# Spreading a first mixture's eighths over an attention loop, and preparing the second mixture as soon as its expert order is known

## Chip, cores and metric

One Trainium2 chip, one of its cores. The metric is the device time of one execution in microseconds; the time before is the median of three runs.

## What is computed

Attention over 4 batches of 8 heads (576 positions, 64 wide) in which each query keeps its 32 largest scores, then a gated feed-forward layer ("the first mixture" below, 512 to 2048 to 512), then a layer of 8 experts ("the second mixture", 512 to 1024 to 512) in which each of the 2304 tokens goes through the one expert that a router picks for it.

```python
scores = scale * np.matmul(q, k.transpose(0, 1, 3, 2))
kth = np.partition(scores, -top_k, axis=-1)[..., -top_k:-top_k + 1]
scores = np.where(scores >= kth, scores, -1000000000.0)
attn = softmax(scores); x = attn @ v                      # -> 2304 x 512
h = x @ w_in; g = h * np.clip(h + 3.0, 0.0, 6.0) / 6.0    # first mixture
x = g @ w_out
expert_idx = np.argmax(xn @ en.T / tau, axis=1)           # router
h = np.maximum(x[mask] @ w1[e], 0.0)                      # second mixture, per expert
out[mask] = gate_w[mask, None] * (h @ w2[e])
```

## The kernel before

Attention runs in 72 units of 128 query rows of two heads (or of left-over rows of four heads: units 8, 13, 26, 31, 44, 49, 62, 63). A software pipeline written by hand takes one **step** (`step`, L751) per unit, 76 in all. In step i, TensorE makes the scores of unit i, VectorE picks the 32 largest of unit i-1 (`select`, the many MAX8 and MATCH_REPLACE8), ScalarE and GpSimd mask and exponentiate units i-2 and i-3, and TensorE transposes unit i-4 and multiplies it with its values (`turned`, `values`). Inside the loop the order of instructions on each engine is the order of the calls in `step`; each engine takes its own in order, and so does the queue of DMA issues on SyncE (the SP queue). The last operation on VectorE that belongs to the scores of a unit is L360, one per step; below, "step s" in a trace is the stretch from the L360 of step s to that of step s+1.

The first mixture is done in groups of one or two 128-token tiles as soon as their attention is finished (`push_group`). The first two groups have one tile, the other eight have two. A group is cut into eight **eighths** of the hidden width, queued in `moe`. An eighth is a first product (L508, 24 matmuls), gate (ScalarE), swish (VectorE, L518), `large` and `small` (a value split in a high and a low part, ScalarE and GpSimd), and a second product (L541, 6 matmuls a tile). Groups become ready in steps 7, 11, 21, 29, 39, 47, 57, 65, 75, and a last group, the left-over rows, after the loop. `step` takes eighths from `moe`: one a step, but two (`a` and `b`) in one step as long as they are of one-tile groups. So before, the one-tile groups run in steps 8 to 15, steps 16 to 21 have no eighth, the two-tile groups run in steps 22-37, 40-55 and 58-73, and steps 38, 39, 56, 57, 74, 75 have none. The last two groups run after the loop.

Weights of the first mixture arrive as 64-bit numbers and are put together from two 32-bit words in 32 conversions (`convert_w`, called by `words` up to four times a step). Each result is split into a high part that stays in SBUF and a low part that is written to DRAM (L218, `lo_dram`) and fetched again for every eighth (`fetch`, L227: 512 KB for each product). A conversion fetches its next raw pieces (L181). Before, steps 0-3 make two conversions each, 4-7 three, 8-10 four.

After a group's second product the tile's rows go to DRAM (`y_dram`, L552) and four small pieces of routing work are queued in `side` (`route`: r1, r2, r4, r5). When 16 of the 18 tiles are routed, `order` (L644 on) ranks the experts by their token counts. `ahead` then prepares the first expert of the second mixture: it loads that expert's token list (`idt`, L692) and weights (L697, L706), gathers its first 256 tokens from `y_dram` (L726, `tokens`), transposes them (L730) and splits the weights (L710, L711). The second mixture follows, with its first product in L901. After the loop the order of instructions is a scheduler's, by simulated times and priorities.

```python
        while moe or last or side:
            if not moe and not rest and "order" in late and "w1" not in late:
                at.close()
                ahead()
            if side:
                with tc.high_priority(offset=SIDE):
                    side.popleft()()
            last = whole(moe.popleft() if moe else None, last)
```

So before, `ahead` is called when the last group's eighths have all been taken, and its gather reads `y_dram` after the last group's rows have been written there.

Of the kernel before, what the change touches and what calls it, by code (L numbers as in the profile page):

```python
# [35 lines left out]
NUNIT = 72  # L36
NS = 4
EARLY = 9
HS = S // 2
QS = S // 4  # L40
SCALE = 1.0 / 8.0
# [2 lines left out]
SIDE = 100  # L44
# [22 lines left out]
def layers(ctx: ExitStack, tc: tile.TileContext, qt, kt, v, w_in, w_out, embt, tau, w1, w2, out, y_dram, g_dram, x_dram, tbl, lo_dram, flag):  # L67
# [71 lines left out]
    def setup():  # L139
        nc.vector.memset(ones, 1.0)  # L140
        nc.vector.memset(acc, 0.0)
        nc.gpsimd.iota(iota8, pattern=[[1, 8]], base=0, channel_multiplier=0, allow_small_or_imprecise_dtypes=True)
        nc.gpsimd.iota(ebase, pattern=[[STRIDE, 8]], base=0, channel_multiplier=0, allow_small_or_imprecise_dtypes=True)
        nc.gpsimd.affine_select(tri, ones, pattern=[[1, 128]], compare_op=ALU.is_gt, fill=0.0, base=0, channel_multiplier=-1)
        nc.gpsimd.iota(ids[:, :, 0], pattern=[[128, NG]], base=0, channel_multiplier=1)
        nc.gpsimd.iota(ids[:, 0:16, 1].rearrange("p (b t) -> p b t", b=4), pattern=[[S, 4], [128, 4]], base=0, channel_multiplier=1)
        for hf in range(2):
            nc.gpsimd.iota(ids[64 * hf:64 * hf + 64, 16:18, 1], pattern=[[2 * S, 2]], base=hf * S + 512, channel_multiplier=1)
        padt = mp.tile([128, E * STRIDE * 2 // 128], I32, tag="ug", name="padt", bufs=4)
        nc.gpsimd.memset(padt, PAD)  # L150
        nc.sync.dma_start(out=tbl.rearrange("(p a) b -> p (a b)", p=128), in_=padt)
        zr = mp.tile([128, DM], F32, tag="ug", name="zr", bufs=4)
        nc.vector.memset(zr, 0.0)
        nc.sync.dma_start(out=y_dram[NT:NT + 1, :], in_=zr[0:1, :])
        for g in (14, 15):
            nc.sync.dma_start(out=y_dram[128 * g:128 * g + 128, :], in_=zr)
        nc.sync.dma_start(out=g_dram[NT:NT + 128, :].rearrange("p o -> o p"), in_=zr[0:1, 0:128])

# [64 lines left out]
    def fetch(n, m):  # L223

        if m < total and m not in lows_[n]:
            lows_[n][m] = t = lop.tile([128, 1024], F32R, tag=f"l{n}", name=f"lo{n}")
            nc.sync.dma_start(out=t.bitcast(F32), in_=lo_dram[n][m % 8])  # L227
# [257 lines left out]
    moe = deque()  # L485
    side = deque()
# [146 lines left out]
    late = {}  # L633
# [118 lines left out]
    def step(i, last):  # L752
# [1 line left out]
            if 0 <= i - j < NU:  # L754
                f(i - j, *a)

        more = iter(range(2 if i < 4 else 3 if i < 8 else 4))

        def words():
            if next(more, None) is not None:  # L760
                convert_w()


        a = moe.popleft() if moe else None
        b = moe.popleft() if moe and a[7] == moe[0][7] == 1 else None
        if last and not last[2]:
            part(last[0], 4)
            part(last[0], 5)
# [30 lines left out]
        at_(3, inverse)  # L799
        if i - 3 >= EARLY:  # L800
            at_(3, scale)
# [27 lines left out]
            setup()  # L829
        if i == 5:  # L830
            embed()
        words()
        return (b, None, False) if b else (a, None, True) if a else None

    if True:
# [18 lines left out]
        last = last[0] if last else None  # L854
        rest = True
        while moe or last or side:
            if not moe and not rest and "order" in late and "w1" not in late:
                at.close()
                ahead()
            if side:  # L860
                with tc.high_priority(offset=SIDE):
                    side.popleft()()
            last = whole(moe.popleft() if moe else None, last)
            if rest and len(moe) <= 1:
                rest = False
                finish_rest()
# [108 lines left out]
        more = nc.values_load(ordi[0:1, 2 * E + 1:2 * E + 2], min_val=0, max_val=NT)  # L975
# [96 lines left out]
```

## Time and profile before

| | |
|---|---|
| median of 3 runs | 1235.53 us (1234.05 to 1240.3) |
| profiled execution | 1232.73 us, span 1230.9 us |
| PE / VectorE / ScalarE / GpSimd busy | 1042.4 / 841.9 / 727.6 / 658.5 us |
| steps 0 to 21 end (L360 of step 22) | 319.7 us |
| L360 of step 71, the last | 789.9 us |
| last matmul of the first mixture issued | 917.29 us |

Times in the trace are microseconds from the span's start. PE is TensorE, DVE VectorE, ACT ScalarE, POOL GpSimd, SPq the DMA queue of SyncE. In a timeline row the bracket tells how long the engine stood idle before the instruction and what ended that; a busy PE is pipelined and its ends are modelled, so it need not be at its peak.

### The profile page before, as it was taken

The numbers are of one execution on the slowest core, as the hardware profiler recorded it, in microseconds if no ns is written. First come the engines' busy times: TensorE is split into PE (matmuls) and PEld (weight loads), VectorE is DVE, ScalarE is ACT, GpSimd is POOL, SyncE is SP. The second block draws the span as 40 slices with busy tenths as digits, with TensorE's granted clock in tenths as the row PEclk, the third lists the DMA queues.
The fourth block names the chain that finished last, engine by engine and source line by source line (L and its number), as shares of the span: only waits on it lengthen the run. The fifth ranks groups of instructions, "written<-read, shape, count | busy, mean of one in ns | idle before, by whom it ended". The sixth has DMA issues, their size and how long they took to land. (4 is left out here: it accounts for less than half of the span.)

```text
span 1230.9 us, 22028 instructions
## 1 busy us (share of the span) xinstructions
PE 1042.4 (85%) x7416; PEld 909.0 (74%) x7416; DVE 841.9 (68%) x2720; ACT 727.6 (59%) x1520; POOL 658.5 (53%) x868
## 2 busy tenths in 40 slices
PE   2333588986999998999998999999976888999993
PEld 1233577974888886888877888879866777888882
DVE  6978576689988999998999898821234343444440
ACT  5656466677777787777887777652333343344540
POOL 6867465577766687766887666642211243122200
PEclk9999878987999998999999999999997999999997
DMA  7645565742433555344454245336670563244530
GB/s 241 200 134 174 195 226 168 230 137 83 145 117 102 170 152 170 83 153 153 119 179 140 86 129 173 112 112 202 190 240 19 170 209 120 85 179 166 184 145 21
DMA packets 99427, 184.98 MB, mean 150 GB/s; under 512 B 21391, under 2 KB 47138, under 8 KB 99295
## 3 DMA queue, kind: packets, MB, share of 16 engines
q1 hardware_dynamic: 94655, 173.29, 43.8%
q0 software_dynamic: 4640, 10.10, 2.5%
q8 instruction: 63, 1.03, 0.4%
q14 instruction: 69, 0.57, 0.2%
HBM read 164.26 MB, written 19.71 MB: 149 GB/s over the span
## 5 line engine op out<-in xcount | busy, mean ns | idle before, releaser
L508 PE MATMUL bank_h<-xh,lo 128*128 128x256 f32 (+1 forms) x640 | 184.7, 289 | 20.7 <-DMA lo<-lo_dram 20.7
L396 POOL TENSOR_TENSOR s<-s,z 128x576 f32<-128x576 f32 x144 | 185.9, 1291 | 11.6 <-ACT z L392 10.0
L508 PE MATMUL bank_h<-xh,vh 128*128 128x256 f32 (+1 forms) x640 | 189.2, 296 | 3.2 <-DVE u L518 3.2
L508 PE MATMUL bank_h<-xl,vh 128*128 128x256 f32 (+1 forms) x640 | 184.4, 288 | 1.1 <-DVE xl L465 1.1
L375 DVE MAX8 A<-left 128x8 f32<-128x288 f32 (+1 forms) x288 | 160.2, 598 | 0.0
L508 PEld LDWEIGHTS bank_h<-xh,lo 128*128 128x128 f32 x640 | 126.8, 198 | 21.4 <-DMA lo<-lo_dram 21.4
L514 ACT ACTIVATE u<-bank_h,half 128x512 f32<-128x512 f32 (+1 forms) x80 | 51.6, 645 | 149.1 <-PE bank_h L508 140.8
L429 PE MATMUL bank_t<-ident,s 128*128 128x128 f32 x648 | 109.2, 298 | 35.6 <-ACT pt L434 12.3
L525 POOL TENSOR_TENSOR gl<-u,gh 128x512 fp32r<-128x512 f32 (+1 forms) x80 | 95.1, 1189 | 80.6 <-ACT gh L522 79.7
L508 PEld LDWEIGHTS bank_h<-xh,vh 128*128 128x128 f32 x640 | 126.6, 198 | 9.0 <-DVE u L518 4.5
L344 PE MATMUL ps_sc<-kst,qh 128*128 128x288 f32 x256 | 88.8, 359 | 51.3 <-ACT s L347 23.2
L508 PEld LDWEIGHTS bank_h<-xl,vh 128*128 128x128 f32 x640 | 126.8, 198 | 1.9 <-DVE xl L465 1.3
L518 DVE SCALAR_TENSOR_TENSOR u<-u,bank_h 128x512 f32<-128x512 f32 (+1 forms) x80 | 50.5, 632 | 110.3 <-ACT u L514 91.1
L541 PE MATMUL y<-lo,gh 128*128 128x512 f32 x288 | 115.4, 401 | 12.4 <-DMA lo<-lo_dram 12.4
L541 PE MATMUL y<-wh,gh 128*128 128x512 f32 x288 | 119.8, 416 | 0.0
L429 PEld LDWEIGHTS bank_t<-ident,s 128*128 128x128 f32 x648 | 78.1, 150 | 52.3 <-ACT pt L434 23.3
L434 ACT COPY pt<-bank_t 128x384 f32<-128x384 f32 x216 | 96.1, 480 | 31.7 <-PE bank_t L429 30.4
L392 ACT ACTIVATE z<-s,zb 128x576 bf16<-128x576 f32 x144 | 112.9, 784 | 1.9 <-DVE zb L381 1.9
L541 PE MATMUL y<-wh,gl 128*128 128x512 f32 x288 | 113.5, 400 | 0.2 <-POOL gl L525 0.2
L402 ACT ACTIVATE s<-s,nb 128x576 f32<-128x576 f32 x144 | 111.9, 777 | 0.0
L711 DVE TENSOR_TENSOR l<-a,h 128x1024 fp32r<-128x1024 f32 x64 | 76.5, 1222 | 50.9 <-ACT h L710 44.3
L447 PE MATMUL bank_a<-pt,vt 128*64 128x128 f32 (+1 forms) x1600 | 104.6, 284 | 0.6 <-ACT pt L434 0.6
(228 smaller groups left out, 2830.0 us busy)
## 6 DMA issues: line engine op xcount, KB each, us to landing
lo<-lo_dram SPq DMA_DIRECT2D x160, 512.0 KB, 4.2
a<-in_moe_w_dram SPq DMA_DIRECT2D x64, 512.0 KB, 7.4
kraw<-in_k_dram SPq DMA_DIRECT2D x64, 144.0 KB, 2.5
qraw<-in_q_dram SPq DMA_DIRECT2D x64, 128.0 KB, 3.2
w<-in_moe_w_in_dram SPq DMA_DIRECT2D x32, 256.0 KB, 3.3
w<-in_moe_w_out_dram SPq DMA_DIRECT2D x32, 256.0 KB, 3.1
lo_dram<-wf SPq DMA_DIRECT2D x32, 256.0 KB, 2.0
vt<-in_v_dram SPq DMA_DIRECT2D x16, 320.0 KB, 3.5
```

The costliest lines, as they stand in the source:

```text
L344: nc.tensor.matmul(ps[:, n, :HS], t, kk[:, HS * g:HS * g + HS], start=(o == 0), stop=(o == len(parts) - 1))
L375: nc.vector.max(A[:, n, 8 * r:8 * r + 8], src[:, n, :w])
L392: nc.scalar.activation(zb_[n], tile_of(i, n), AF.Relu, bias=sel[i][2][:, n:n + 1], scale=-BIG)
L396: nc.gpsimd.tensor_tensor(s, s, zb_[n], op=ALU.subtract)
L402: nc.scalar.activation(s, s, AF.Exp, bias=sel[i][1][:, n:n + 1], scale=SCALE, accum_out=sums[i][:, n:n + 1])
L429: nc.tensor.transpose(pp[:, 128 * k:128 * k + 128], e[:, 128 * (3 * c + k):128 * (3 * c + k) + 128], ident)
L434: nc.scalar.copy(pts[i][:, 3 * c:3 * c + 3, :].rearrange("p k n -> p (k n)"), tb_.pop((i, c))[:, :384])
L447: nc.tensor.matmul(av[64 * n:64 * n + 64, c0:c1], vt[:, k, 64 * n:64 * n + 64], pt[:, k + 5 * n if k < 4 else 4, c0:c1], start=(o == 0), s ...
L508: nc.tensor.matmul(ph[:, a, :], w, x[:, k, :], start=(k == 0 and n == 0), stop=(k == 3 and n == 2))
L525: nc.gpsimd.tensor_tensor(state[q][1], state.pop((q, "u")).rearrange("p (a n) -> p a n", a=2), state[q][0].bitcast(F32), op=ALU.subtract)
L541: nc.tensor.matmul(state["y"][o], x[:, a, c], w, start=(f == 0 and n == 0), stop=(f == 15 and n == 2))
L711: nc.vector.tensor_tensor(lo, x, hi.bitcast(F32), op=ALU.subtract)
```

## The change

A table of steps replaces the rule by group size: one eighth a step, two in steps 18 and 20, none in steps 26, 35, 44, 53, 62, 71. The one-tile groups then run in steps 8 to 21, and the others in steps 22-30 (less 26), 31-39 (less 35), and so on to 75. Conversions go at 2, 2, 3 in turn, and end in step 13. The first two fetches are made in step 6. After the loop two pieces of routing are taken per turn in place of one, and `ahead` is called as soon as the order is known, while eighths are still queued; the zeros that `y_dram` is given at the start are now in tiles 16 and 17, the last group's.

```diff
+PAUSE = tuple(range(26, 72, 9))
+TWO = (18, 20)
...
-        for g in (14, 15):
+        for g in (16, 17):
             nc.sync.dma_start(out=y_dram[128 * g:128 * g + 128, :], in_=zr)
...
-        more = iter(range(2 if i < 4 else 3 if i < 8 else 4))
+        more = iter(range(3 if i % 3 == 2 else 2))
...
-        a = moe.popleft() if moe else None
-        b = moe.popleft() if moe and a[7] == moe[0][7] == 1 else None
+        a = moe.popleft() if moe and i not in PAUSE else None
+        b = moe.popleft() if i in TWO else None
...
+        if i == 6:
+            fetch(0, 0)
+            fetch(1, 0)
...
-            if not moe and not rest and "order" in late and "w1" not in late:
+            if not rest and "order" in late and "w1" not in late:
                 at.close()
                 ahead()
-            if side:
-                with tc.high_priority(offset=SIDE):
-                    side.popleft()()
+            for _ in range(2):
+                if side:
+                    with tc.high_priority(offset=SIDE):
+                        side.popleft()()
```

The rows below are those of the built programs; the changed one has line numbers larger by 3 in this part of the program and by 6 behind the loop (L230 is L227 of before, L221 L218, L184 L181, L298 L295, L511 L508, L521 L518, L544 L541, L714 L711, L733 L730, L907 L901).

**The SP queue, steps 6 to 8.** Before (`lo_dram_61` holds the low parts of w_in, `lo_dram_62` those of w_out):

```order
L181 DMA w_1076<-in_moe_w_in_dram 128x512
L181 DMA w_1078<-in_moe_w_out_dram 128x512
L295 DMA qraw<-in_q_dram 128x2x128
L218 DMA lo_dram_62<-wf 128x512
L227 DMA lo_1120<-lo_dram_61 128x1024
L227 DMA lo_1146<-lo_dram_61 128x1024
L181 DMA w_1160<-in_moe_w_out_dram 128x512
L181 DMA w_1162<-in_moe_w_out_dram 128x512
L181 DMA w_1199<-in_moe_w_out_dram 128x512
L181 DMA w_1201<-in_moe_w_in_dram 128x512
```

Changed:

```order
L184 DMA w_915<-in_moe_w_out_dram 128x512
L221 DMA lo_dram_62<-wf 128x512 x2
L298 DMA qraw<-in_q_dram 128x2x128
L230 DMA lo_961<-lo_dram_61 128x1024
L230 DMA lo_963<-lo_dram_62 128x1024
L184 DMA w_989<-in_moe_w_out_dram 128x512
L184 DMA w_991<-in_moe_w_out_dram 128x512
L184 DMA w_1024<-in_moe_w_out_dram 128x512
L184 DMA w_1026<-in_moe_w_in_dram 128x512
L221 DMA lo_dram_61<-wf 128x512 x2
```

The first fetches of both low parts stood behind the last write of step 7 and in step 8; they now stand behind step 6's loads of the queries, ahead of a whole step's loads and writes.

**PE, the last group of the first mixture.** Before, its last second product, routing, and the transposes of the gathered tokens `xg`:

```order
L541 MATMUL y<-wh,gl 128x512 x2
L541 MATMUL y<-wh,gh 128x512
L541 MATMUL y<-lo_11154,gh 128x512
L541 MATMUL y<-wh,gl 128x512
L570 MATMUL bank_t_124<-ident,ysb 128x128 x4
L730 MATMUL bank_t_123<-ident,xg 128x128 x8
L901 MATMUL ph_11357<-xh__11234,h_11252 128x256
```

Changed, first around the second product of the last eighth but two (`lo_11155`), then at the start of the last but one's (`lo_11202`):

```order
L511 MATMUL bank_h<-xl,vh 128x256
L511 MATMUL bank_h<-xh,lo_11134 128x256
L733 MATMUL bank_t_123<-ident,xg 128x128 x4
L544 MATMUL y<-wh,gh 128x512 x2
L544 MATMUL y<-lo_11155,gh 128x512
L544 MATMUL y<-wh,gl 128x512
L544 MATMUL y<-wh,gh 128x512
L544 MATMUL y<-lo_11155,gh 128x512
```

```order
L511 MATMUL bank_h<-xl,vh 128x256
L511 MATMUL bank_h<-xh,lo_11181 128x256
L544 MATMUL y<-wh,gh 128x512 x2
L544 MATMUL y<-lo_11202,gh 128x512
L544 MATMUL y<-wh,gl 128x512
L907 MATMUL ph_11357<-xh__11077,h_11095 128x256
L907 MATMUL ph_11372<-xh__11077,h_11095 128x256
L544 MATMUL y<-wh,gh 128x512
```

The transposes of the gathered tokens moved ahead of the second products of the last three eighths, and 24 matmuls of the second mixture's first product now stand among the last of the first mixture's. The order's matmul (L644) moved ahead by 10 matmuls of a first product and the 12 of a second one.

**VectorE, the same place.** Before (L659 writes the expert order, L711 splits the expert's weights):

```order
L659 CAST ordi<-res 1x8
L518 SCALAR_TENSOR_TENSOR u<-u,bank_h 128x512
L711 TENSOR_TENSOR l_11253<-a_11229,h_11252 128x1024
L518 SCALAR_TENSOR_TENSOR u<-u,bank_h 128x512
L711 TENSOR_TENSOR l_11253<-a_11229,h_11252 128x1024 x3
L518 SCALAR_TENSOR_TENSOR u<-u,bank_h 128x512
L732 TENSOR_TENSOR xl__11235<-bank_t_123,xh__11234 128x4x128 x2
```

Changed:

```order
L662 CAST ordi<-res 1x8
L714 TENSOR_TENSOR l_11096<-a_11072,h_11095 128x1024
L521 SCALAR_TENSOR_TENSOR u<-u,bank_h 128x512
L714 TENSOR_TENSOR l_11096<-a_11072,h_11095 128x1024 x3
L521 SCALAR_TENSOR_TENSOR u<-u,bank_h 128x512
L735 TENSOR_TENSOR xl__11078<-bank_t_123,xh__11077 128x4x128 x2
L521 SCALAR_TENSOR_TENSOR u<-u,bank_h 128x512
```

The split of the weights stood ahead of the swishes of the last two eighths; it now stands ahead of those of the last three.

## Rows read from the trace of the kernel before

**Rows 1.** The page's part 2: busy tenths in 40 slices of 30.8 us.

```profile
PE   2333588986999998999998999999976888999993
...
DVE  6978576689988999998999898821234343444440
```

**Rows 2.** Windows: steps 0-6, 7-13, 14-21; length, engines' busy (x instructions), PEclk, DMA share, GB/s.

```profile
17.40:113.40 96.00, 38.70 (x182) 30.62 (x182) 88.80 (x287) 61.91 (x133) 69.83 (x93) 1.00 0.55 181
113.40:243.00 129.60, 96.93 (x695) 89.14 (x697) 84.53 (x282) 70.72 (x161) 71.95 (x94) 0.87 0.61 202
243.00:319.70 76.70, 59.38 (x462) 49.69 (x463) 70.15 (x258) 58.37 (x136) 54.97 (x80) 0.82 0.40 122
```

**Rows 3.** Waits of 75 to 260 us: total us, times, longest.

```profile
DVE u L518 <- ACT u L514: 19.9, 6, 12.9
...
PE bank_h L508 <- DMA lo<-lo_dram: 19.6, 3, 15.1
```

**Rows 4.** Timeline of 121 to 127 us, SP queue and PE: start, us, what, idle before.

```profile
121.56 0.92 SPq L227 DMA_DIRECT2D lo<-lo_dram  x2
...
126.32 0.48 PE L508 MATMUL bank_h<-xh,lo 128*128 128x128 f32 x1 [15.14 <-DMA lo<-lo_dram]
```

**Rows 5.** Groups of VectorE, 17.4 to 319.7 us: count, busy us, mean ns, idle before.

```profile
L199 DVE TENSOR_SCALAR wf<-w 128x256 int32<-128x256 int32 x60 | 33.1, 592 | 0.0
...
L201 DVE SCALAR_TENSOR_TENSOR wf<-w,wf 128x256 int32<-128x256 int32 x60 | 24.1, 441 | 0.0
...
L518 DVE SCALAR_TENSOR_TENSOR u<-u,bank_h 128x256 f32<-128x256 f32 x16 | 6.7, 418 | 39.0 <-ACT u L514 19.9 <-issue 18.8
...
L207 DVE SCALAR_TENSOR_TENSOR wf<-w,wf 128x256 int32<-128x256 int32 x15 | 6.2, 414 | 0.0
```

**Rows 6.** Timeline of PE: the twenty matmuls of one unit's values, early and later.

```profile
108.15 2.40 PE L447 MATMUL bank_a<-pt,vt 128*64 128x128 f32 x20
...
382.89 1.31 PE L447 MATMUL bank_a<-pt,vt 128*64 128x128 f32 x20
```

**Rows 7.** Window of steps 11-14, two one-tile eighths in each.

```profile
205.30:254.70 49.40, 49.17 (x432) 45.41 (x434) 35.08 (x132) 32.26 (x74) 25.88 (x42) 1.00 0.61 193
```

**Rows 8.** Timeline of PE near 898 us: first product, second product, next first product.

```profile
895.29 0.36 PE L508 MATMUL bank_h<-xh,vh 128*128 128x256 f32 x1
...
898.25 0.40 PE L541 MATMUL y<-wh,gh 128*128 128x512 f32 x1
...
901.00 0.28 PE L508 MATMUL bank_h<-xh,vh 128*128 128x256 f32 x1
```

**Rows 9.** Windows of steps 26, 35 and 38.

```profile
356.20:365.80 9.60, 9.60 (x77) 8.37 (x76) 8.32 (x32) 7.14 (x17) 6.28 (x10) 1.00 0.40 130
443.30:455.10 11.80, 11.80 (x97) 10.56 (x97) 11.43 (x38) 9.67 (x23) 8.72 (x13) 1.00 0.69 206
...
473.70:481.20 7.50, 6.06 (x35) 4.82 (x35) 7.47 (x30) 4.49 (x12) 5.17 (x9) 0.55 0.24 82
```

**Rows 10.** Timeline of PE, end of the first mixture to the second's first matmuls.

```profile
895.25 0.18 PE L644 MATMUL bank_a<-acc,ones 128*128 128x8 bf16 x1
...
908.39 0.39 PE L508 MATMUL bank_h<-xh,vh 128*128 128x256 f32 x1 [1.61 <-DVE u L518]
...
917.52 0.60 PE L570 MATMUL bank_t<-ident,ysb 128*128 128x128 f32 x4
...
927.54 1.08 PE L730 MATMUL bank_t<-ident,xg 128*128 128x128 f32 x4 [9.42 <-DMA xg<-y_dram,idt]
...
936.44 0.95 PE L578 MATMUL bank_t<-ent,yt 128*128 128x8 f32 x8
```

**Rows 11.** Timeline of the same stretch: SP queue, ScalarE, GpSimd.

```profile
899.13 0.41 SPq L692 DMA_DIRECT2D idt<-tbl  x1
...
905.43 1.05 ACT L710 CAST h<-a 128x1024 fp32r<-128x1024 f32 x1 [4.79 <-DMA a<-in_moe_w_dram]
...
924.04 0.99 POOL L726 DMA_INDIRECT xg<-y_dram,idt  x1 [8.52 <-DMA y_dram<-ysb]
```

## The prediction

> **What bounds the kernel now.** I read the slices of the page first, then windows cut at the L360 of a step, then the waits of the stretch that stood out, and last the timeline at the end of the first mixture. [rows 1] shows three regimes. In the first ten slices (308 us) VectorE is at 5 to 9 tenths and TensorE at 2 to 9, neither full. From there to slice 29 TensorE is full almost throughout. In slices 30 and 31 TensorE falls to 7 and 6 tenths with VectorE at 3 and 4, so neither bounds it: something is waited for.
>
> In the first regime VectorE is the nearest to a bound, and [rows 2] shows where it is held up: in steps 0-6 it is busy for 88.8 of 96.0 us, in 14-21 for 70.2 of 76.7, but in steps 7-13 for 84.5 of 129.6 us only. [rows 3] names the reason: VectorE's swishes waited for the gate, the gate for the first product, and that for the low part of the weights, 15.1 us in one piece. [rows 4] shows that piece: the fetch was issued at 121.56 us, behind the writes of its queue, when TensorE already stood at the matmul that needs it, and the matmul began at 126.32. With two eighths in a step each later fetch is also wanted half a step after it is asked for.
>
> **Steps 0 to 21.** Nothing of VectorE's work goes away; it is moved. One conversion costs VectorE (33.1 + 24.1 + 6.2) us / 30 = 2.1 us, one swish of a one-tile eighth 0.42 us [rows 5]. I go by stretches.
> - Steps 0-6: one conversion fewer, 96.0 - 2.1 = 93.9 us. The waits that remain there (the expert embedding in step 5) are not touched.
> - Steps 7-13: 84.5 us of VectorE, one conversion more, six swishes fewer: 84.5 + 2.1 - 2.5 = 84.1 us, or 12.0 a step. The early fetch removes the long wait, and since each eighth asks for the next one's parts a whole step ahead, I cost the other fetches at nothing: the cover is a step of 12 us against the 4.8 us from issue to matmul in [rows 4].
> - TensorE in these steps: an eighth of a two-tile group takes 901.00 - 895.29 = 5.7 us [rows 8], and a step with one takes 9.6 us when TensorE never stops [first of rows 9], so a step without takes 3.9. Four steps with two one-tile eighths took 49.4 us with TensorE always busy [rows 7]: (49.4 / 4 - 3.9) / 2 = 4.2 us for one. A step with one is then 8.1 us, under VectorE's 12.0.
> - That holds at the higher clock. The same twenty matmuls took 2.40 us at 108 us and 1.31 us at 383 us [rows 6]: although the window says 1.00 for steps 0-6 [rows 2], TensorE runs there at the lower of its two levels, and 7-13 had a granted clock of 0.87. At the lower level a step with one eighth takes 8.1 x 1.83 = 14.8 us, 2.8 more than VectorE's. I take half of the six steps 8-13 at that level: 8 us, with 0 and 17 as ends, because a TensorE that is the bound is busy all the time, and where it was so it had the full clock [rows 7].
> - The Trainium skill, in "TensorE: Matmul & The Clock Gate" (What's actually happening), says that the throttled state is the default and that activity lifts it. The slow matmuls of [rows 6] agree with that, and the 1.00 of the window does not; by the window this term would be 0 and the whole forecast 8 us lower.
> - Steps 14-21: eight swishes more, 70.2 + 3.3 = 73.5 us, 9.2 a step. Steps 18 and 20 carry two eighths: 3.9 + 2 x 4.2 = 12.3 us on TensorE, 3.1 more each. Sum 79.7 us.
>
> The L360 of step 22 comes at 17.4 + 93.9 + 84.1 + 8 + 79.7 = 283 us in place of 319.7: **36.6 us less**. The work of GpSimd in steps 7-13, 72 us [rows 2], and of ScalarE, 71, changes by little and stays under 84; SP's order of writes and loads is the same but for the fetches.
>
> **Steps 22 to 75.** 48 eighths in 54 steps before and now; only the six empty steps move. Step 26 was bound by TensorE, 9.60 us; without its eighth's first product it falls to VectorE's 8.32 less a swish (at least 0.42): 1.7 us less. The step behind a pause has a first product but no second, so it too falls to VectorE: 1.3 less by the same row. Step 35 was long on both, 11.80 against 11.43 us, and gains 0.8. Step 38, empty before at 7.50 us, becomes a step of 9.6: 2.1 more [rows 9]. Step 39 had its successor's first product already and stays. The sum is 1.7 us for 18 steps; over three such stretches, the last of which ends in the drain, I take **4 us less** (from 3 more to 9 less: TensorE is full for most of these steps, and a pause leaves it idle wherever it stands).
>
> **The end of the first mixture.** Before, the order's matmul was at 895.25, the last second product ended by 917.52, and then TensorE stood 9.42 us for the gathered tokens [rows 10]: GpSimd's gather had itself waited 8.52 us for the last rows to land in `y_dram` [rows 11]. It then made the transposes and 24 first-stage matmuls until 936.44. The gather now needs only the token list, loaded 3.9 us after the order's matmul [rows 11], so this wait goes. What is late next is the split of the expert's weights: ScalarE's first cast of them waited 4.79 us until 905.43 [rows 11], 10.2 us after the order's matmul, and held up a swish and with it TensorE for 1.61 us [rows 10].
>
> Counted from the order's matmul, TensorE's own work was 917.52 - 895.25 - 1.6 = 20.7 us. That matmul now stands 10 x 0.12 + 12 x 0.23 = 4.0 us of work earlier (a first product is 2.96 us for 24, a second 2.75 for 12 [rows 8]), so 24.7 us. Moved in are two sets of transposes (at most 1.1 us) and the 24 first-stage matmuls (as much as a first product, 2.9). The wait for the split grows, since it now stands ahead of three swishes: the first cast comes 10.2 us plus about 0.6 behind the order's matmul, then a cast, gate, split and swish of some 3 us, 13.8 in all, while TensorE wants that swish after 4.0 + 5.6 = 9.6 us of work: 4.2 us of waiting. Sum: 24.7 + 1.1 + 2.9 + 4.2 + 0.6 for the routing's transposes = 33.5 us from 891.25, hence 924.7 against 936.44: **11.7 us less**, 16 if the weights cost no wait, 5 if they wait twice as long and the last low part, queued behind the second weights, adds 2. All that follows (counts, lists, the other seven experts) hangs on this stretch and keeps its length.
>
> **Sum.** 36.6 + 4 + 11.7 = 52.3 us. The profiled execution took 1232.7, so 1180.4; the median of the runs shown is 2.8 above that execution, so I predict **1183 us** for the median.
>
> **Rivals.**
> - The weights of the first expert give the end back (chance 0.10): the loads now run beside the low parts of three eighths and the wait of 4.2 us becomes 16. For it: a cast already waits for them [rows 11]. Against it: these loads stand ahead of the fetches in the queue. Time 1195.
> - The low parts are still late (0.07). If two or three waits of steps 7-13 stay, as would follow from writes that hold up the queue, 20 us come back: 1203. Against it: the 15 us wait was one fetch asked for too late [rows 4].
> - The lower clock holds for half of steps 8-21 (0.07). At the lower level twelve of them take 14.8 us and two 22.5, that is 223 us in place of 160, 63 more; half of that makes 1214.
> - Slower than before (0.04): the lower clock holds throughout steps 8-21, because the even spread leaves TensorE short gaps in every step where it had eight full ones before. 63 us more make 1246. It decides against the change once more than 52 / 63, five sixths, of that excess is there. The granted 0.82 of steps 14-21 [rows 2], where TensorE had little to do, speaks for it; the full clock at full load [rows 7] against it.
>
> **Numbers.** The forecast has 0.72, from 1166 (full clock throughout, 16 us at the end) to 1195. The range 1166 to 1209 takes in the first two rivals and leaves out the others. About 0.5%, 6 us, can be told from no change. Faster 0.94: all but the last rival and a sliver of the third; within 0.5%: 0.02; slower: 0.04.
>
> **What would show it.** Right: the L360 of step 22 near 283 us, VectorE busy for more than nine tenths of steps 7-13, no wait of `bank_h` for `lo` above 2 us there, the gather of `xg` issued before the last L541, and 24 L901 done some 30 us behind the order's matmul. Wrong: L360 of step 22 beyond 300, matmuls at the lower level through steps 8-21, or TensorE idle for more than 8 us for the weights' split at the end.

## The result, and the profile after

The changed kernel took **1198.21 us** (median of 4 runs, 1195.13 to 1202.4) against 1234.79 beside it: a ratio of 0.9697, 95% interval 0.9651 to 0.9743. The forecast was 1183, with a range from 1166 to 1209: right in direction, 15 us too fast. The profiled execution took 1195.13 us, its span 1193.2. In the text, L360, which marks the steps, and L914, the second product of the second mixture, are named by the kernel before; in the changed one they are L363 and L920.

The page's part 2 of the changed kernel, to be laid beside [rows 1] (40 slices of 29.8 us):

```profile
PE   2247778999999899999899999999998898999993
...
DVE  6979998979998998898898898711234343444440
...
PEclk9965877999999899999899999999999898999997
```

TensorE is now at 8 tenths or more from the seventh slice on (the eleventh before), and the two slices of 7 and 6 tenths at the end of the first mixture are gone.

Windows of steps 0-6, 7-13 and 14-21, which answer to [rows 2] (length, busy us of PE, PEld, DVE, ACT, POOL, PEclk, DMA share, GB/s):

```profile
16.90:111.00 94.10, 39.70 (x189) 32.05 (x189) 86.43 (x283) 60.89 (x131) 67.46 (x90) 0.76 0.57 186
111.00:197.80 86.80, 67.90 (x492) 59.98 (x492) 83.86 (x273) 65.46 (x150) 72.69 (x90) 0.81 0.64 205
197.80:283.30 85.50, 79.94 (x647) 72.98 (x648) 72.38 (x261) 61.65 (x147) 58.58 (x85) 0.92 0.59 191
```

Steps 7-13 shrank from 129.6 to 86.8 us, of which VectorE is busy for 83.9; steps 14-21 grew from 76.7 to 85.5 and are now nearer to TensorE's bound. The L360 of step 22 comes at 283.3 in place of 319.7.

Waits of 75 to 260 us (total us, times, longest), against [rows 3], and the first fetch with what follows it, against [rows 4]:

```profile
DVE u L521 <- ACT u L517: 5.7, 4, 3.1
...
PE bank_h L511 <- DMA lo<-lo_dram: 7.3, 6, 2.4
```

```profile
103.22 0.97 SPq L230 DMA_DIRECT2D lo<-lo_dram  x2
...
109.24 0.41 PE L511 MATMUL bank_h<-xh,lo 128*128 128x128 f32 x1
```

The 15.1 us wait is gone: the fetch is issued 6.0 us before the matmul that needs it, which waits for nothing. The longest wait for a low part in steps 7-13 is now 1.5 us; the one of 2.4 stands in step 14, and four such waits, 5.1 us together, fall in steps 14-21.

The end of the first mixture, timelines of TensorE, then of the SP queue, ScalarE and GpSimd, against [rows 10] and [rows 11]:

```profile
868.69 0.18 PE L647 MATMUL bank_a<-acc,ones 128*128 128x8 bf16 x1
...
880.18 0.39 PE L511 MATMUL bank_h<-xh,vh 128*128 128x256 f32 x1 [1.65 <-DVE u L521]
...
883.90 0.63 PE L733 MATMUL bank_t<-ident,xg 128*128 128x128 f32 x4 [0.58 <-DMA xg<-y_dram,idt]
...
899.25 0.40 PE L544 MATMUL y<-wh,gl 128*128 128x512 f32 x1
...
916.10 0.17 PE L596 MATMUL bank_t<-oh,tri 128*128 128x8 bf16 x1 [4.37 <-DVE oh L590]
```

```profile
872.84 0.41 SPq L695 DMA_DIRECT2D idt<-tbl  x1
...
877.22 1.06 ACT L713 CAST h<-a 128x1024 fp32r<-128x1024 f32 x1 [4.82 <-DMA a<-in_moe_w_dram]
...
876.37 0.99 POOL L729 DMA_INDIRECT xg<-y_dram,idt  x1 [2.61 <-DMA a<-in_moe_w_dram]
```

The gather stands at 876.37, 22.9 us ahead of the last second product, and TensorE waits 0.58 us for the gathered tokens where it waited 9.42.

Where the time went, from the profiled executions: up to step 22, 36.4 us less. From there to the first eighth that runs alone after the loop, **14.1 us more** (510.2 to 524.3). From that place to the end of the span, 15.4 us less (401.0 to 385.6). The sum, 37.7 us, is the difference of the spans (1230.9 to 1193.2). The middle was forecast at 4 less: 18.1 us of error there, more than the whole miss of 15, since the end gave 3.7 more than forecast. The experiments turn on the middle.

### The profile page after: what moved, and what is told of

Its sections match the earlier page's. It is cut to its first block, busy times and chain, and to the rows that moved or that the text cites. A ratio compares the mean times of both kernels' runs of the same rounds, so it can differ in the third digit from the quotient of the medians.

```text
span 1193.2 us, 22013 instructions
## 1 busy us (share of the span) xinstructions
PE 1036.8 (87%) x7416; PEld 905.5 (76%) x7416; DVE 839.0 (70%) x2720; ACT 726.2 (61%) x1520; POOL 662.9 (56%) x868
## 5 line engine op out<-in xcount | busy, mean ns | idle before, releaser
L399 POOL TENSOR_TENSOR s<-s,z 128x576 f32<-128x576 f32 x144 | 188.9, 1312 | 14.7 <-ACT z L395 14.0
L511 PE MATMUL bank_h<-xh,lo 128*128 128x256 f32 (+1 forms) x640 | 184.3, 288 | 8.0 <-DMA lo<-lo_dram 8.0
L511 PE MATMUL bank_h<-xh,vh 128*128 128x256 f32 (+1 forms) x640 | 188.8, 295 | 1.7 <-DVE u L521 1.7
L511 PE MATMUL bank_h<-xl,vh 128*128 128x256 f32 (+1 forms) x640 | 183.6, 287 | 1.2 <-DVE xl L468 1.0
L511 PEld LDWEIGHTS bank_h<-xh,lo 128*128 128x128 f32 x640 | 125.9, 197 | 9.0 <-DMA lo<-lo_dram 9.0
L511 PEld LDWEIGHTS bank_h<-xh,vh 128*128 128x128 f32 x640 | 125.5, 196 | 6.9 <-issue 2.4
L511 PEld LDWEIGHTS bank_h<-xl,vh 128*128 128x128 f32 x640 | 125.8, 197 | 2.3 <-DVE xl L468 1.8
L544 PE MATMUL y<-wh,gh 128*128 128x512 f32 x288 | 121.0, 422 | 0.0
L437 ACT COPY pt<-bank_t 128x384 f32<-128x384 f32 x216 | 96.3, 481 | 37.7 <-PE bank_t L432 37.4
L714 DVE TENSOR_TENSOR l<-a,h 128x1024 fp32r<-128x1024 f32 x64 | 76.7, 1224 | 56.1 <-ACT h L713 55.8
L544 PE MATMUL y<-lo,gh 128*128 128x512 f32 x288 | 115.6, 401 | 0.4 <-DMA lo<-lo_dram 0.4
L544 PE MATMUL y<-wh,gl 128*128 128x512 f32 x288 | 114.0, 400 | 0.0
L521 DVE SCALAR_TENSOR_TENSOR u<-u,bank_h 128x512 f32<-128x512 f32 (+1 forms) x80 | 50.6, 633 | 86.4 <-ACT u L517 86.4
L450 PE MATMUL bank_a<-pt,vt 128*64 128x128 f32 (+1 forms) x1600 | 101.5, 278 | 0.6 <-ACT pt L437 0.6
```

The source lines that it names most:

```text
L399: nc.gpsimd.tensor_tensor(s, s, zb_[n], op=ALU.subtract)
L437: nc.scalar.copy(pts[i][:, 3 * c:3 * c + 3, :].rearrange("p k n -> p (k n)"), tb_.pop((i, c))[:, :384])
L450: nc.tensor.matmul(av[64 * n:64 * n + 64, c0:c1], vt[:, k, 64 * n:64 * n + 64], pt[:, k + 5 * n if k < 4 else 4, c0:c1], start=(o == 0), s ...
L511: nc.tensor.matmul(ph[:, a, :], w, x[:, k, :], start=(k == 0 and n == 0), stop=(k == 3 and n == 2))
L544: nc.tensor.matmul(state["y"][o], x[:, a, c], w, start=(f == 0 and n == 0), stop=(f == 15 and n == 2))
L714: nc.vector.tensor_tensor(lo, x, hi.bitcast(F32), op=ALU.subtract)
```

## The experiments

Twelve kernels were run. The kernel before had medians from 1233.84 to 1234.62 us beside them. Except where a diff is against the kernel before, the edit is to the changed kernel.

### Three parts, one at a time

Theory 1: the early part gives some 36 us, the end some 15, and the six empty steps ("pauses") cost some 14. Theory 2: the pauses cost nothing, and the 14 us come of the early part, whose work would be carried over into the middle.

**Without the pauses.**

```diff
-PAUSE = tuple(range(26, 72, 9))
+PAUSE = ()
```

> The change without its table of empty steps: one eighth a step from step 22 on, as before the change, so that steps 38, 39, 56, 57, 74, 75 are the empty ones again. Theory 1 (the early part gave 36 us, the end 15 us, and the six empty steps inside the loop took 14 back): 1184 us, 14 below the changed kernel, with the stretch from the L360 of step 22 to the first eighth that runs by itself after the loop back at 510 us. Theory 2 (the 14 us are carried over from the early part, the table costs nothing): 1198 us and 524 us.

Measured: 1178.94 us (1176.2 to 1179.8), ratio 0.9557 (0.9526 to 0.9588). It beats both kernels, the changed one by 19.3 us in the medians and by 16.6 in the two traces' spans, and lies 5 us below what theory 1 said.

**The early part alone**: the kernel before with one eighth a step, the even pace of conversions and the early fetch.

```diff
-        more = iter(range(2 if i < 4 else 3 if i < 8 else 4))
+        more = iter(range(3 if i % 3 == 2 else 2))
...
-        b = moe.popleft() if moe and a[7] == moe[0][7] == 1 else None
+        b = moe.popleft() if i in TWO else None
...
+        if i == 6:
+            fetch(0, 0)
+            fetch(1, 0)
```

> Before plus the early part alone (two eighths only in steps 18 and 20, conversions 2, 2, 3, fetches in step 6). Theory 1: 36 us below before, 1199 us, and L360 of step 22 at 283 us. Theory 2: the later stretch is longer by 14 us although its empty steps are as before, 1213 us.

Measured: 1195.99 us (1192.31 to 1196.75), ratio 0.9688 (0.9656 to 0.972); the stretch from step 22 to the first lone eighth is 510.2 us, as before. Nothing is carried over.

**The pauses alone**, in the kernel before:

```diff
-        a = moe.popleft() if moe else None
+        a = moe.popleft() if moe and i not in PAUSE else None
```

> Before plus the table of empty steps alone. Theory 1: 14 us slower than before, 1249 us. Theory 2: 1235 us, as before.

Measured: 1243.83 us (1243.48 to 1245.67), ratio 1.0091 (1.0061 to 1.0121): slower, by 9.2 us, with 523.5 us for the same stretch.

**The end alone**: the kernel before with `ahead` as soon as the order is known and two pieces of routing a turn.

```diff
-        for g in (14, 15):
+        for g in (16, 17):
...
-            if not moe and not rest and "order" in late and "w1" not in late:
+            if not rest and "order" in late and "w1" not in late:
...
-            if side:
-                with tc.high_priority(offset=SIDE):
-                    side.popleft()()
+            for _ in range(2):
+                if side:
+                    with tc.high_priority(offset=SIDE):
+                        side.popleft()()
```

> Before plus the end alone (zeros in tiles 16 and 17, two pieces of routing a turn, the second mixture prepared once the order is known). Theory 1: 15 us below before, 1220 us. Rival (part of the end's gain came from what the other parts shifted): 1225 to 1230 us.

Measured: 1218.9 us (1218.19 to 1222.71), ratio 0.9882 (0.9854 to 0.9911).

What follows: Theory 2 falls. Early part and end give 38.6 and 15.7 us, and 1234.6 - 38.6 - 15.7 = 1180.3 is the kernel without pauses to 1.4 us. The pauses cost 9.2 us alone and 19.3 in the changed kernel. The traces show where these two figures differ: from step 22 to the first lone eighth the pauses alone cost 13.3 us (523.5 against 510.2), and those of the changed kernel 11.4 (524.3 against 512.9 without them). The rest lies mostly in the second mixture: counted from its first L914 to the end, it was 4.7 us shorter with the pauses alone than in the kernel before (274.0 against 278.7), though its instructions stand in the same order there on all four compute engines, and 5.0 longer in the changed kernel than without pauses (276.6 against 271.6), where the scheduler has moved some of them.

### What the pauses cost, and where

**Only the first four, only the last two.**

```diff
-PAUSE = tuple(range(26, 72, 9))
+PAUSE = (26, 35, 44, 53)
```

> The changed kernel with the first four pauses (26, 35, 44, 53) and without 62 and 71. Theory: a pause costs wherever it stands in the loop, some 3 us each in the changed kernel (19 us for six), because the step behind it has no other product to put between its scores and the waits for GpSimd and ScalarE. Then 1179 + 4 x 3.2 = 1192 us, ratio 0.965. Rival: only the last pair costs, since the kernel before had its last two empty steps in the drain behind the last scores, where they are free; then 1179 to 1182 us. The place of the first lone eighth behind the loop (512.9 us behind the start of step 22 without pauses, 524.3 with all) at 520 by the theory, 513 to 514 by the rival.

```diff
-PAUSE = tuple(range(26, 72, 9))
+PAUSE = (62, 71)
```

> The changed kernel with the last two pauses (62, 71) alone. Theory (each pause costs alike): 1179 + 2 x 3.2 = 1185 us, first lone eighth 517 us behind the start of step 22. Rival (the last pair carries nearly all): 1192 to 1198 us, 523 us.

Measured: 1193.59 us (1189.78 to 1199.32) with the four, 1189.52 (1186.52 to 1199.09) with the two; ratios 0.9663 (0.9613 to 0.9713) and 0.9659 (0.9606 to 0.9712). Both are slower than without pauses, but the medians don't price the pauses: in both traces the second mixture is longer than the 271.6 us without pauses, by 8.0 us with the four (279.6) and by 6.8 with the two (278.4). The first lone eighth came 520.9 us behind step 22 with the four, as the theory had it, but 514.1 with the two, where 517 and 523 were expected: steps 58 to the first lone eighth are 5.4 us longer than without pauses (169.2 against 163.8), but the two stretches ahead of them, the same program in both kernels, were 4.3 us shorter (172.9 + 172.0 against 175.9 + 173.3).

All 14 traces together tell more than two of them. The stretches, in us, of the kernels that have these pauses and of those that have none there (the pauses two steps later left out):

| stretch | without (10 traces) | with (3 traces) |
|---|---|---|
| steps 22-39 (pauses 26, 35) | 171.7 to 175.9 | 172.9 to 175.6 |
| steps 40-57 (44, 53) | 172.0 to 173.5 | 178.3 each |
| step 58 to the first lone eighth (62, 71) | 163.8 to 167.0 | 169.2 to 172.3 |
| of that, behind the L360 of step 71 | 39.9 to 40.0 | 46.7 to 47.7 |

So the second pair cost 4.8 to 6.3 us and the third 2.2 to 8.5, outside the scatter of these traces; what the first pair costs is lost in it.

**Two steps later**, off the left-over units (26, 44, 62 are such units):

```diff
-PAUSE = tuple(range(26, 72, 9))
+PAUSE = tuple(range(28, 74, 9))
```

> The changed kernel with the six pauses two steps later, 28, 37, 46, 55, 64, 73, so that none falls on a left-over unit, whose low query part GpSimd prepares only one step ahead. If the three waits of 1.72 us for that part make the cost together with what they push back, 1198 - 5 = 1193 us, and no wait of the scores for `zq` is left in the trace. The last pause, 73, also falls behind the last scores: another 2 to 3 us less, 1190. Rival (any empty step costs the same, wherever it stands): 1198. Second rival (the cost is in pauses that split the eighths of a group apart in the trough of the groups' ends): 37 and 55 stand where the kernel without pauses has its empty steps too, so about two thirds of the 19 us go: 1185.

Measured: 1186.92 us (1184.43 to 1189.17), ratio 0.9609 (0.9573 to 0.9646): 11.3 us less than the changed kernel, nearest to the second rival; 7.9 us of that are in the stretch from step 22 to the first lone eighth (516.4 against 524.3). The waits for `zq` are gone. These are, among the waits of TensorE in that stretch, those of its scores and of its longest fetch, in the changed kernel and in this one:

```profile
PE ps_sc L347 <- ACT s L350: 5.5, 5, 1.1
PE ps_sc L347 <- POOL zq L328: 5.2, 3, 1.7
...
PE bank_h L511 <- DMA lo<-lo_dram: 0.7, 1, 0.7
```

```profile
PE ps_sc L347 <- ACT s L350: 5.5, 5, 1.1
PE bank_h L511 <- DMA lo<-lo_dram: 3.5, 2, 2.6
```

and one of the three in the changed kernel's timeline, at the end of step 25, where the pause has taken away the first product that stood ahead of these scores:

```profile
313.85 1.20 PE L347 MATMUL ps_sc<-kst,zq 128*128 128x288 f32 x7 [1.72 <-POOL zq L328]
```

What the loop does with a pause is best seen in windows of the four stretches steps 22-39, 40-57, 58-70, and from the L360 of step 71 to the first lone eighth. First the kernel before, then the changed one, then the one with the pauses two steps later:

```profile
319.70:491.50 171.80, 166.27 (x1342) 144.44 (x1342) 159.12 (x571) 133.03 (x296) 124.89 (x173) 0.98 0.45 141
491.50:665.00 173.50, 167.13 (x1357) 145.30 (x1356) 162.30 (x585) 134.37 (x299) 127.51 (x177) 0.99 0.45 140
665.00:789.90 124.90, 124.90 (x1029) 109.53 (x1027) 112.24 (x414) 93.43 (x204) 88.03 (x123) 1.00 0.39 123
789.90:829.90 40.00, 37.02 (x298) 32.09 (x298) 16.05 (x67) 21.91 (x49) 19.53 (x28) 1.00 0.34 115
```

```profile
283.30:457.50 174.20, 166.71 (x1330) 144.55 (x1330) 158.81 (x575) 132.58 (x294) 126.34 (x175) 0.97 0.44 136
457.50:635.80 178.30, 169.54 (x1356) 146.77 (x1356) 161.61 (x585) 134.49 (x299) 127.78 (x177) 0.97 0.44 136
635.80:759.90 124.10, 120.66 (x998) 104.90 (x998) 112.45 (x417) 93.11 (x204) 86.24 (x122) 1.00 0.40 126
759.90:807.60 47.70, 44.34 (x348) 38.77 (x346) 14.62 (x59) 24.06 (x52) 21.28 (x28) 1.00 0.44 133
```

```profile
281.20:453.40 172.20, 164.54 (x1330) 142.53 (x1330) 158.87 (x575) 133.02 (x294) 126.16 (x175) 0.99 0.43 137
453.40:629.10 175.70, 168.17 (x1357) 146.66 (x1356) 160.99 (x585) 134.94 (x299) 127.64 (x177) 0.98 0.43 138
629.10:751.50 122.40, 121.29 (x1010) 106.34 (x1010) 112.98 (x419) 93.30 (x203) 86.87 (x122) 1.00 0.42 133
751.50:797.60 46.10, 42.86 (x335) 37.20 (x333) 14.48 (x58) 24.24 (x53) 20.52 (x28) 1.00 0.38 124
```

Read the last two lines of the first two blocks together. The kernel before ran 62 first and 53 second products by step 71, the changed one 60.5 and 52 (its matmuls counted at L508 and L541, by 24 and by 12, so that the second product of a one-tile eighth counts half). So 1.5 x 2.96 + 2.75 = 7.2 us of TensorE's work [rows 8] was left for the drain behind them, which grew by 7.7 us. Steps 58-70 became only 0.8 us shorter in exchange, though TensorE was busy there for 4.2 us less: never idle before, it now stood idle for 3.4 us. Before, the group's two empty steps were 74 and 75, which lie in the drain, where a step without an eighth is simply short. The kernel with the pauses two steps later agrees: it ran 61 and 52 by step 71, which leaves 2.96 + 2.75 = 5.7 us more for the drain, and its drain took 46.1 us, 6.1 more.

In steps 40-57 the work is the same in both kernels and the time 4.8 us longer. Windows of the steps round each pause show that they aren't alike: steps 25-29, 34-37, 43-47 and 52-55, in the kernel before and in the changed one (pauses 26, 35, 44, 53).

```profile
346.20:394.30 48.10, 48.10 (x400) 42.25 (x400) 41.65 (x152) 35.84 (x79) 32.70 (x46) 1.00 0.39 118
433.40:473.70 40.30, 37.32 (x311) 31.71 (x309) 39.58 (x138) 35.44 (x84) 34.21 (x47) 1.00 0.56 173
518.50:567.50 49.00, 49.00 (x409) 43.14 (x409) 43.67 (x162) 35.80 (x79) 33.96 (x48) 1.00 0.37 117
606.60:647.00 40.40, 37.68 (x311) 31.71 (x309) 39.71 (x138) 34.88 (x82) 34.22 (x47) 1.00 0.54 167
```

```profile
311.10:356.60 45.50, 42.60 (x359) 36.75 (x358) 41.87 (x153) 33.43 (x74) 32.55 (x46) 1.00 0.37 108
396.20:438.90 42.70, 38.45 (x297) 33.17 (x296) 39.99 (x137) 32.67 (x77) 34.14 (x47) 0.88 0.47 143
486.30:534.80 48.50, 45.60 (x373) 39.59 (x372) 43.95 (x163) 34.74 (x78) 33.94 (x48) 0.96 0.36 102
574.30:617.40 43.10, 37.53 (x303) 31.98 (x302) 40.62 (x137) 33.54 (x78) 34.26 (x47) 0.92 0.48 143
```

Round the pauses at 26 and 44, where TensorE was the bound, the steps do become shorter, by 2.6 and 0.5 us, but by 2.9 us less each than TensorE's busy time falls: nearly all of that is a wait of 1.72 us for `zq` and one of 1.11 for ScalarE's copy of the scores. Round those at 35 and 53 they become longer, by 2.4 and 2.7 us, though TensorE has fewer matmuls. The steps 35, 36 and 37 alone, in the changed kernel:

```profile
407.30:416.70 9.40, 6.16 (x40) 4.75 (x39) 9.30 (x33) 8.87 (x21) 8.41 (x12) 0.70 0.62 172
416.70:429.00 12.30, 12.30 (x83) 11.07 (x84) 11.37 (x39) 7.93 (x20) 7.91 (x11) 0.81 0.55 172
429.00:438.90 9.90, 9.90 (x80) 8.67 (x80) 9.72 (x34) 7.95 (x19) 9.20 (x14) 1.00 0.45 154
```

Step 35 does fall to VectorE's time, from 11.80 us [rows 9] to 9.40. But TensorE is idle for 3.2 us in it, and its granted clock is 0.70, and the next step runs at 0.81 and takes 12.3 us where step 36 took 9.35 before. The clock is not all of that: step 36 starts 26 matmuls of first products now and started 7 before. Step 54, behind the pause at 53, took 12.58 us against 9.36, at a granted 1.00 in both, with 37 of these matmuls against 18.

The idle time and the clock can be told apart over the whole stretch, step 22 to the first lone eighth, since the matmuls in it are the same but for a few missing records (us; windows of that stretch):

| kernel | length | TensorE idle | TensorE busy | granted clock |
|---|---|---|---|---|
| before | 510.2 | 14.9 | 495.3 | 0.99 |
| early part alone | 510.2 | 16.5 | 493.7 | 1.00 |
| without pauses | 512.9 | 14.1 | 498.8 | 0.98 |
| changed | 524.3 | 23.1 | 501.2 | 0.98 |
| pauses two steps later | 516.4 | 19.5 | 496.9 | 0.99 |
| pauses alone | 523.5 | 21.1 | 502.4 | 0.97 |

Of the 14.1 us that the changed kernel lost against the kernel before, 8.2 are idle time, among them the 5.2 of the waits for `zq`, and 5.9 are a longer busy time for the same matmuls, which goes with the lower clock. The second part is the less certain one: the early part alone and the kernel without pauses run the same program in this stretch, and 5.1 us of busy time lie between them.

### One routing piece ahead of all

```diff
-SIDE = 100
+SIDE = 500
```

(on the kernel without pauses.)

> The changed kernel without pauses, and with the routing pieces of the last tiles ahead of all other work (SIDE 500 in place of 100). In the changed kernel the last routing matmul of the second mixture comes 5.4 us behind the last first-stage matmul that stands ready, before 0.2 us. If that routing is late because its VectorE work waits behind the split of the second weights, up to 5 us go: 1174 us, ratio to the kernel without pauses 0.996. Rival: it waits for the tokens' transposes, which the priority does not change: 1179.

Measured: 1191.03 us (1185.9 to 1193.98), ratio 0.9632 (0.9588 to 0.9676): 12 us slower than without it. A miss for both: the last routing matmul no longer trails, but the 96 first-stage matmuls it should have overlapped end 9.2 us later (908.3 against 899.1), and the second mixture behind them is longer too, 282.9 us from its first L914 to the end against 271.6. Among the 96, TensorE stands idle for 4.63 us before 905.79, for VectorE's L910 (L904 in the kernel before), which VectorE starts at 905.32, right behind its last split of the second weights (L714). Most of what the second mixture adds is one row. TensorE's longest entry among the waits of the second mixture, in the kernel before, without pauses, and with the routing first:

```profile
PE pxt L730 <- DMA xg<-y_dram,idt: 12.8, 7, 4.3
```

```profile
PE pxt L733 <- DMA xg<-y_dram,idt: 7.1, 3, 2.9
```

```profile
PE pxt L733 <- DMA xg<-y_dram,idt: 15.7, 7, 5.0
```

The same gathers of tokens are waited for 3 to 7 times. The length of the second mixture varied with it among all kernels run: the shortest wait and length are those without pauses, the longest those with the routing first, and the other twelve lie between (8.6 to 13.3 us of waits, 274.0 to 280.5 of length). Why the gathers come when they do stays open. It bears on the 19.3 us between the changed kernel and the one without pauses: in the two traces the stretch from step 22 to the first lone eighth accounts for 11.4 us of it (524.3 to 512.9) and the second mixture for 5.0 (276.6 to 271.6).

### What makes up the early part

**The even spread and pace without the early fetch** (on the kernel without pauses):

```diff
-        if i == 6:
-            fetch(0, 0)
-            fetch(1, 0)
```

> The changed kernel without pauses and without the early fetch of step 6. Theory 1: the 15.1 us wait for the first low part comes of that fetch alone, the spread cannot hide it, so some 13 us come back, 1179 + 13 = 1192 us, and the L360 of step 22 stands at 296. Theory 2: with one eighth in a step the first eighth's swish is the only thing that waits, while VectorE goes on with conversions that stood in its place anyway; 1179 to 1184 us and L360 of step 22 at 284 to 288.

Measured: 1203.71 us (1202.86 to 1207.14), ratio 0.9772 (0.9738 to 0.9806). L360 of step 22 at 303.6.

**The early fetch alone**, in the kernel before (the same three lines added):

> The kernel before with the early fetch in step 6 and nothing else. Theory 1: the wait of 15.1 us goes and little else: 1234.6 - 13 = 1221 us, L360 of step 22 near 307. Theory 2: two eighths in a step keep the steps 7 to 13 bound by the later fetches and by TensorE's lower clock, so that only 3 to 6 us of it are won: 1229 to 1232 us.

Measured: 1216.92 us (1214.71 to 1223.71), ratio 0.989 (0.9848 to 0.9931). L360 of step 22 at 302.7.

**The spread alone**, in the kernel before (the line with `TWO` alone):

> The kernel before with one eighth in each of the steps (two in 18 and 20 only) and nothing else: neither the early fetch nor the even pace of the conversions. Theory 1: 38.6 us of the early part less the 13 of the fetch and some 2 of the pace: 1234.6 - 24 = 1211 us, L360 of step 22 near 297. Theory 2 (the spread carries nearly all): 1199 us, 285.

Measured: 1222.37 us (1221.12 to 1225.83), ratio 0.9919 (0.9887 to 0.9951). L360 of step 22 at 307.3: a miss for both theories.

Against 319.7, then, the fetch alone wins 17.0 us of the loop, the spread alone 12.4, spread and pace together 16.1, all three 36. The expectations put the fetch too low: with spread and pace in place it is worth 20 us (303.6 less 283.8), and the rest of what the median of 1203.71 has over 1178.94 is the second mixture again, 279.3 us against 271.6, less 3.9 us of the stretch from step 22 to the first lone eighth (509.0 against 512.9). TensorE's waits of 17 to 300 us without the fetch show the reason:

```profile
PE bank_h L511 <- DMA lo<-lo_dram: 15.2, 6, 8.9
...
PE y L544 <- DMA lo<-lo_dram: 12.3, 1, 12.3
```

The fetch brings the low parts of both products, and the second product waits for its own. Beside the 15.1 us of the first product that the forecast went by, the kernel before had three waits of 12.4 us together at L541 too, 9.3 and 3.0 of them in steps 7-13; in the changed kernel they are 0.4 us in the whole trace. The fetch alone leaves five waits of 2.1 to 2.7 us in steps 7-13.

### `ahead` early, but one piece a turn

The end alone, without its `for _ in range(2)`:

> The kernel before with the second mixture prepared as soon as the order is known, but one routing piece a turn as before. With two pieces a turn this part gave 15.7 us (1218.9). If the gain is the gather that no longer waits for the last rows, and the two pieces a turn only bring the order's matmul 4 us earlier, 15.7 - 4 = 12 us are left: 1223 us. Rival: the order known two eighths later pushes the weights' split and the first gather to the end of the first mixture, so that most of the 15.7 us goes: 1230.

Measured: 1234.25 us (1231.1 to 1239.67), ratio 1.0003 (0.9985 to 1.0021): **nothing** is left. The rival holds, and more than it said. The order's matmul, the list's load and the gather in this kernel:

```profile
899.38 0.18 PE L647 MATMUL bank_a<-acc,ones 128*128 128x8 bf16 x1
```

```profile
903.26 0.41 SPq L695 DMA_DIRECT2D idt<-tbl  x1
```

```profile
928.51 0.99 POOL L729 DMA_INDIRECT xg<-y_dram,idt  x1 [9.65 <-DMA y_dram<-ysb]
```

The load of the token list is issued at 903, but the gather still waits 9.65 us for the last rows: one routing piece a turn makes the order known only in the turn in which the last eighth is taken, so the early condition is met no earlier than the old one. The two traces show it: all instructions of the four compute engines, and SyncE's DMA issues, stand in the same order as in the kernel before, so but for the tiles that are zeroed at the start this is the same program. That makes its profile a measure of scatter as well: 1237.8 us of span against 1230.9. In the kernel with the end part whole the order's matmul is at 892.73 and the gather at 900.40. The condition and the two pieces a turn are one edit; the condition alone is worth nothing, and the two pieces alone weren't tried.

## Why the prediction was right, and where it was not

- **What bounded the kernel**: right in the main. Steps 7-13 were held up by late low parts, and VectorE bounds them without these (83.9 of 86.8 us busy). But it was not one fetch: the forecast named the 15.1 us of the first product and not the 9.3 and 3.0 us of the second products (L541), and the fetch alone won 17.0 us of the 36.
- **Steps 0 to 21**: forecast 36.6 us, 36.4 in the trace, 38.6 as a median with this part alone. Its parts were less exact. Steps 0-6 took 94.1 us (forecast 93.9), steps 7-13 86.8 (forecast 92.1: 84.1 and 8 for the lower clock), steps 14-21 85.5 (forecast 79.7). In the later steps TensorE is busy for 79.9 of those 85.5 us at a granted 0.92, where I had reckoned with the full clock, and it waits 5.1 us for low parts, which I had costed at nothing; how much each adds isn't shown. An error of 5 us less and one of 6 more cancel: that the sum came out so near is luck.
- **The end**: forecast 11.7 us; 13.3 in the trace from the first lone eighth to the first L914 (122.3 to 109.0) and 2.1 behind it; 15.7 as a median with this part alone. The gather's wait went as said. What is late next was named rightly but priced too high: the first cast of the weights came 8.5 us behind the order's matmul and not 10.8, and held TensorE up by 1.65 us, not 4.2. Not foreseen: the last tile's routing now trails the first-stage matmuls by 4.4 us. VectorE's splits of the second weights (L714) stand before it from 909.56 to 914.2; that the 24 matmuls that moved ahead no longer cover it is argued from the order alone.
- **Steps 22 to 75**: this is the step that failed: "I take 4 us less". It came out 14.1 us more in the trace, and 9.2 (alone) to 19.3 us (in the changed kernel) in the medians. Its stretch of 18 steps was to fall by 1.7 us. Against the early part alone, which has the same steps without pauses, the changed kernel took 1.3 us more in steps 22-39, 5.8 more in 40-57 and 7.0 more from there to the first lone eighth. Three things in its working were wrong. That "the last of which ends in the drain" was counted as one more stretch of gain; in truth the kernel before had its last two empty steps in the drain, where they are free, and the change pushes 7.2 us of products into it. That a step with a pause falls to VectorE's time and the next one does too was wrong at the second pause of a stretch: step 35 fell by 2.4 us, more than the 0.8 reckoned, but step 36 rose by 3.0. And the gain at one pause was taken for all: step 26 was to fall to 7.9 us and took 9.59, yet steps 25 to 29 together fell by 2.6, near the 3.0 reckoned for steps 26 and 27; at the pause at 44 the same five steps fell by only 0.5, and those round the pause at 53 rose by 2.7. My own remark that a pause leaves TensorE idle wherever it stands was right and should have set the sign of the term.
- **Rivals**: that the weights give the end back, that the low parts are still late, and that the lower clock holds for half or all of steps 8-21 did not occur. The cost of the pauses, which did, was in none of them. That the time lies inside the range all the same is luck: its upper end, 1209, was made for two rivals that did not occur, and without them it was 1195.

How much of the pauses' cost is idle time of TensorE and how much the lower clock is settled for the whole stretch only, and by single traces; moving the pauses two steps took away 3.5 us of idle time and 4.4 of busy time at once. Whether the pauses do anything to the second mixture stays open.

## What to carry to other kernels

An empty slot in a software pipeline is worth something only where the engine that it relieves is the bound of that slot and stays covered by other work; where the work is pushed on into a drain that runs on that engine alone, it costs its full length (here 7.2 us of work left at the last step, and 7.7 us more of drain). Count the work that has left a loop by its last step in both kernels before pricing a shift. A condition that starts work earlier gains nothing until what it waits for really comes earlier: here the test and the doubled routing were worth 15.7 us together, and the test alone 0.

## What was not expected of the hardware

- The granted clock of a window says 1.00 until the first recorded change. [rows 2] gave 1.00 for steps 0-6 of the kernel before, the changed kernel 0.76 for the same steps, and the twenty matmuls of one unit's values took 2.40 us at 96.71 us in the changed kernel as in [rows 6]:

```profile
96.71 2.40 PE L450 MATMUL bank_a<-pt,vt 128*64 128x128 f32 x20
```

  So the matmuls' own durations are the safer reading early in a trace. The 0.87 of steps 7-13 in [rows 2] is too high for the same reason: from 113.4 to 133.1 us the window of the kernel before says 1.00, while the 128x128 matmuls of its first product (L508, 126.8 us on) start 0.21 us apart, against 0.11 in the changed kernel at 122 us.
- What a drop of the clock costs depends on where it falls, and the same step differs by 3 us with it. Step 38, empty in both, had a granted clock of 0.55 in the kernel before [rows 9] and 0.56 without the pauses. These are the windows of step 39 behind it, before and without the pauses, with the same products in it:

```profile
481.20:491.50 10.30, 9.19 (x84) 8.43 (x85) 9.93 (x37) 7.58 (x17) 5.95 (x9) 1.00 0.59 200
```

```profile
446.50:459.70 13.20, 12.09 (x83) 11.51 (x83) 9.51 (x37) 7.51 (x17) 5.93 (x9) 0.73 0.48 155
```

- The Trainium skill, in "TensorE: Matmul & The Clock Gate" (What's actually happening), calls the throttled state the default, which activity lifts. The windows of steps 35 to 37 agree (0.70 in the step with 3.2 us of idle TensorE, 0.81 in the busy one behind it, then 1.00), and the 2.40 us of the early matmuls above do too.
